# FFT and SwiGLU kernel: first-batch loads over two queues, sign and weight passes on ScalarE, and extra TensorE work between the first stages

## The chip, the cores and the metric

The kernel runs on one core of one Trainium2 chip. The metric is the device time of that core in microseconds (us). Times are medians over fast runs. Every run of a kernel was compared with runs of the kernel before on the same chip in the same rounds. Below, `before` is the kernel before the change and `after` is the changed kernel.

The first profile that I had of `before` shows TensorE at half its rate: consecutive 512-column matmuls start 443 ns apart in it.

## The reference

```python
# x: (8, 3008, 256) f32;  w_gate, w_val: (256, 1536) f32;  w_out: (1536, 256) f32
X = np.fft.fft(np.fft.fft(x, axis=1), axis=2).real.astype(np.float32)
t = X.reshape(8 * 3008, 256)
g = t @ w_gate
out = ((g / (1 + np.exp(-g))) * (t @ w_val)) @ w_out      # (24064, 256) f32
```

## The kernel before

The kernel computes the sequence transform as matmuls with cosine and sine tables (`Tab`). It multiplies the transform over the feature dimension into the gate and value weights instead of applying it to the data. So the start-up has to make two things before the main stage can begin: the first transformed tile (`Pt`, `Qt`) and the first transformed weights (`Wp`, `Wq`, `Wm`). The main stage is then one long sequence of gate, value and output matmuls.

The tables have symmetries, so rows of x are first added to and subtracted from their mirror rows. "Rising" rows are read in order and "falling" rows are their mirrors. Of the first batch, set A has 128 rows of each kind in four column groups (`XA`, rising in 0:4 and falling in 4:8). Set C has the remaining 60 in two halves of the partitions (`XC0`), plus the two single rows that are loaded by one small DMA. A permutation matmul in f32 (`place`) lines the rising rows up with the falling ones. VectorE then makes the sums and differences (`sums`), GpSimd folds A's columns (`fold_d`) and ScalarE rounds them to bf16 (`EOb`). TensorE multiplies with the tables (`half_folded` for A, `unfolded` for C).

The loads, on two queues. `nc.sync` is the engine that the profile calls SP:

```python
    nc.vector.memset(zero, 0.0)
    nc.vector.memset(sel, 0.0)
    nc.scalar.activation(halfpi, zero, AF.Silu)
    xf = XC0.rearrange("p a q d -> p (a q d)")
    nc.scalar.copy(xf, zero.to_broadcast([P, xf.shape[1]]))
    q.dma_start(out=XA3[:, 0:4, :], in_=up_block(0, 1, P))
    for a in (3, 2, 1, 0):
        q.dma_start(out=XA3[:, 4 + a, :], in_=down_set(0, a, JA, LA, NA))
    for hi, eng in ((1, nc.scalar), (0, q)):
        eng.dma_start(out=XC3[64 * hi:64 * hi + NCR, 0:2, :],
                      in_=rows_at(0, 2 * (P + 1) - 1 + 2 * hi * R, [[2 * D, NCR], [R * D, 2], [1, 2 * D]]))
        for a in range(2):
            eng.dma_start(out=XC3[64 * hi:64 * hi + NCR, 2 + a, :],
                          in_=down_set(0, 3 - 2 * hi - a, JC, LC, NC_))
    q.dma_start(out=XC0[NCR:64 + NCR + 1:64, 0:2, 1],
                in_=rows_at(0, 0, [[2 * R * D, 2], [R * D, 2], [1, D]]))
# ... then four small DMAs on SP that copy zeros within XC
```

The opening matmuls, the passes over the tables and the tables of the feature transform:

```python
    for i in range(4):
        ps = psO.tile([P, T], F32, name="o")
        for j in range(12):
            nc.tensor.matmul(ps[:, 0:P], sel, sel, start=True, stop=True)
# ...
    def weigh(lo, hi):
        vts(Tab[:, 1, 1, :, lo:hi], Tab[:, 1, 1, :, lo:hi], scalar1=wC, scalar2=None, op0=Alu.mult)

    def opposite(ch):
        vts(Tab[:, ch, :, :, NCE:NOO - 1], Tab[:, ch, :, :, GH + 1:NCE], scalar1=-1.0, scalar2=None, op0=Alu.mult)
# ...
    def d_tables():
        magnitude(rad, rrd)
        nc.scalar.activation(CD, rad, AF.Sin, scale=-scd, bias=halfpi)
        nc.scalar.activation(SDt, rrd, AF.Sin, scale=-scd, bias=zero)
        nc.scalar.activation(CD[:, :, 0:1], CD[:, :, 0:1], AF.Copy, scale=0.5)
```

Placing, sums, folds, first table matmuls and the weight products:

```python
    def place(X, put, n, pools):
        pss = []
        for a in range(n):
            pool, nm = pools[a % len(pools)]
            ps = pool.tile([P, 2, D], F32, name=nm)
            nc.tensor.matmul(ps.rearrange("p q d -> p (q d)"), put, X[:, a].rearrange("p q d -> p (q d)"),
                             start=True, stop=True)
            pss.append(ps)
        return pss

    def sums(S, k, X, pss):
        n = len(pss)
        for a in range(n):
            down = X[:, 7 - a] if n == 4 else X[:, 2 + a]
            vtt(S[:, k, a], pss[a], down[:, ::-1, :], op=(Alu.add, Alu.subtract)[k])
# ...
    def half_folded(eo, a0):
        for q in range(2):
            for a in range(a0, a0 + 2):
                dst, rhs = set_cols(acc[eo][q], Tab[:, 0, q, eo], a)
                nc.tensor.matmul(dst, EOb[:, eo, a, q, :], rhs, start=(a == 0), stop=False, skip_group_check=True)
# ...
    def fold_d(eo, a0):
        s_ = SA[:, eo, a0:a0 + 2]
        ptt(EOA[:, eo, a0:a0 + 2, :, 0:P], s_[:, :, :, P:0:-1], s_[:, :, :, P:D], op=(Alu.add, Alu.subtract)[eo])
        nc.scalar.copy(EOb[:, eo, a0:a0 + 2], EOA[:, eo, a0:a0 + 2, :, 0:P])
# ...
    def transform_w(fc, gv, k, ps):
        dst, tab = ((Wp, CD), (Wq, SDt))[k]
        src = W0[gv] if fc == 0 else Wraw[gv][:, :, (fc - 1) * T:fc * T]
        fs = slice(fc * T, (fc + 1) * T)
        for no in range(2):
            nc.tensor.matmul(ps, tab[:, no, :], src[:, no, :], start=(no == 0), stop=(no == 1))

        def copies():
            if k:
                nc.scalar.copy(dst[:, gv, fs], ps)
                if fc == 1:
                    nc.scalar.activation(Wm[:, gv, fs], ps, AF.Copy, scale=m2)
                else:
                    pts(Wm[:, gv, fs], dst[:, gv, fs], scalar1=m2, scalar2=1.0, op0=Alu.mult, op1=Alu.mult)
            else:
                nc.vector.tensor_copy(dst[:, gv, fs], ps)
        return copies
```

The order in which the start-up is written:

```python
    psA = place(XA, putA, 4, ((psG, "g"), (psV, "v")))
    sums(SA, 0, XA, psA)
    opposite(0)
    for a in (0, 2):
        fold_d(0, a)
    sums(SA, 1, XA, psA)
    start_acc(0)
    for a in (0, 2):
        half_folded(0, a)
        fold_d(1, a)
    psC = place(XC0, putC, 2, ((psO, "o"),))
    load_w(1)
    d_tables()
    weigh(0, NCE)
    opposite(1)
    sums(SC, 0, XC0, psC)
    halves(SBc, SC, 0)
    start_acc(1)
    for a in (0, 2):
        half_folded(1, a)
    hd = tp.tile([P, 2, 2, 1], F32, name="hd")
    ptt(hd, SA[:, 0, 0:2, :, 0:1], SA[:, 0, 2:4, :, 0:1], op=Alu.add)
    heads(nc.gpsimd, hd[:, 0], hd[:, 1], CEa)
    nc.gpsimd.tensor_copy(EOA[:, 0, :, :, P:P + 1], SA[:, 0, :, :, 0:1])
    heads(nc.gpsimd, SC[:, 0, 0, :, 0:1], SC[:, 0, 1, :, 0:1], CEc)
    sums(SC, 1, XC0, psC)
    halves(SBc, SC, 1)
    nc.vector.memset(SDt[:, :, 0:1], 1.0)
    load_w(2)
# ...
    def weights0(gv):
        for k in range(2):
            ps = psO.tile([P, T], F32, name="o")
            fn = transform_w(0, gv, k, ps)
            if gv and not k:
                nc.scalar.copy(Wp[:, gv, 0:T], ps)
            else:
                fn()

    unfolded(0, SBc)
    transform(0, 0, (0,), acc)
    weights0(0)
    for q in range(2):
        row0(0, q, acc[1][q])
    unfolded(1, SBc)
    transform(0, 0, (1,), acc, lambda: weights0(1))
```

## Time and profile before

| | before |
|---|---|
| time, median of fast runs | 626.35 us |
| first profile (TensorE at half rate): span | 1250.8 us |
| second profile (full rate; the same kernel, run later as a control): span | 624.9 us |
| first gate matmul of the main stage, second profile | 28.21 us |
| TensorE busy, second profile | 97% |

These lines are of the page of the first profile of `before`: its span, the busy time of each engine, and the TensorE clock that was granted in 40 equal slices of the span, in tenths.

```profile
span 1250.8 us, 12575 instructions
...
PE 1243.1 (99%) x4068; PEld 583.1 (47%) x4068; DVE 604.0 (48%) x1045; ACT 561.4 (45%) x996; POOL 454.1 (36%) x421
...
PEclk9999999999999999999999999999999998555555
```

The span is twice the timed median, and consecutive 512-column matmuls start 443 ns apart. The clock row says nines for the most part (the mean granted clock is 0.931), so it does not show this state. The prediction was made from this profile, by halving TensorE's times.

The control run of `before` gave a profile at full rate. Everything below compares it with the full-rate profile of `after`.

```profile
span 624.9 us, 12515 instructions
...
PE 606.9 (97%) x4008; PEld 394.6 (63%) x4068; DVE 570.2 (91%) x1045; ACT 524.5 (84%) x996; POOL 453.7 (73%) x421
...
PEclk8799999999999999999999999999999999999999
```

(The page counts 60 matmuls fewer than weight loads, where most other pages count the same: some matmul records are missing, here after the start-up. The page of `after` lacks 60 too.) Two slices of the start-up are not at full clock. The timeline of TensorE shows what happens there. The columns are start (us), duration (us), engine, line, operation, output and inputs, shapes and count; the bracket is the idle time just before and what ended it. This is `before`, full rate.

```profile
12.86 0.81 PE L440 MATMUL v<-Tab,EOb 128*128 128x377 bf16 x2 [2.75 <-ACT EOb L453]
...
17.44 3.75 PE L403 MATMUL o<-XC,putC 128*128 128x512 f32 x4 [1.89 <-DMA XC<-in_x_dram]
20.99 0.84 PE L440 MATMUL v<-Tab,EOb 128*128 128x377 bf16 x2
...
22.74 0.48 PE L440 MATMUL g<-Tab,EOb 128*128 128x377 bf16 x2
...
28.21 0.37 PE L871 MATMUL g<-Pt,Wp 128*128 128x480 bf16 x1
```

The placing of C (L403) waited 1.89 us for a DMA and then took 3.75 us. From 12.3 to 22.6 us TensorE ran at half rate: a pair of table matmuls takes 0.84 us there and 0.48 us afterwards.

Which DMA did C's placing wait for? This is the timeline of SP's queue (SPq: time in which SP issues DMAs) in the same profile.

```profile
6.38 0.40 SPq L245 DMA_DIRECT2D XC<-in_x_dram  x1
7.35 5.11 SPq L248 DMA_DIRECT2D XC<-in_x_dram  x2
12.51 0.59 SPq L250 DMA_DIRECT2D XC<-in_x_dram  x1
```

Why it waited for just that load can be read from the packed trace, which holds the semaphore on which each load signals its landing. In those of `before` and `after` the twelve loads of A and C use eight semaphores. The ninth to the twelfth load each use the semaphore of an earlier load again, and SP waits for that semaphore before each of them. In `before` the single rows are the twelfth load. In the new order they are the eighth, the last one that needs no such wait.

VectorE's timeline in the same profile:

```profile
12.00 0.38 DVE L340 TENSOR_SCALAR Tab<-Tab 128x752 bf16<-128x752 bf16 x1
...
14.89 1.27 DVE L337 TENSOR_SCALAR Tab<-Tab,wC 128x754 bf16<-128x754 bf16 x1
...
19.53 0.69 DVE L412 TENSOR_TENSOR SC<-o,XC 128x512 f32<-128x512 f32 x1 [2.75 <-PE o L403]
```

The sign and weight passes (L340, L337) stand between the sums (L412). Yet VectorE then stood idle for 2.75 us before C's first sum, because of the placing. In this order the passes were not what C's sums waited for.

### The profile page before, as it was taken

How to read it: one execution, taken by the hardware profiler on the slowest of the kernel's cores; microseconds unless marked ns; L12 is line 12 of the kernel's file. 1: busy time of each engine (PE TensorE's matmuls, PEld its weight loads, DVE VectorE, ACT ScalarE, POOL GpSimd, SP SyncE). 2: the span in 40 equal slices, each digit the busy share in tenths (PEclk: the TensorE clock that was granted, in tenths of full speed). 3: DMA queues.
4: the chain of work that ended last, by engine and by line, in shares of the span. 5: the costliest groups of instructions: out<-in, count | busy, mean ns of one | idle time of the engine just before them, and what ended most of it. 6: DMA issues, size and time to landing. Idle time of an engine off the chain costs nothing.

```text
span 1250.8 us, 12575 instructions
## 1 busy us (share of the span) xinstructions
PE 1243.1 (99%) x4068; PEld 583.1 (47%) x4068; DVE 604.0 (48%) x1045; ACT 561.4 (45%) x996; POOL 454.1 (36%) x421
## 2 busy tenths in 40 slices
PE   9999999999999999999999999999999999999998
PEld 4334444444444444444444444444444444545465
DVE  6543234445444554445444544545544455555552
ACT  4433223444444445444454444544445444555552
POOL 6535212343342444523434334343343221332231
PEclk9999999999999999999999999999999998555555
DMA  8312321213013002121021100103000000101011
GB/s 179 56 28 69 78 71 46 70 43 72 28 34 77 26 27 67 51 73 47 18 73 42 30 22 17 48 25 90 22 21 27 17 30 22 31 26 31 29 34 39
DMA packets 50237, 57.39 MB, mean 46 GB/s; under 512 B 7170, under 2 KB 37226, under 8 KB 50154
## 3 DMA queue, kind: packets, MB, share of 16 engines
q1 hardware_dynamic: 46701, 53.73, 16.0%
q0 software_dynamic: 3184, 2.36, 1.3%
q10 hardware_dynamic: 285, 0.49, 0.2%
q8 instruction: 32, 0.52, 0.2%
q14 instruction: 35, 0.29, 0.1%
HBM read 29.39 MB, written 24.65 MB: 43 GB/s over the span
## 4 chain that ended last, share of the span: by engine, by line
PE 99%; issue 1%; ACT 0%; POOL 0%; DVE 0%; ACTq 0%
PE o L1077 40%; PE g L871 28%; PE v L871 22%; PE o L1236 2%; PE g L1236 2%; PE o L461 1%; PE o L281 0%; PE g L549 0%; PE o L549 0%; PE v L403 0%; PE o L403 0%; PE g L403 0%; PE g L447 0%; PE v L447 0%; PE g L440 0%
## 5 line engine op out<-in xcount | busy, mean ns | idle before, releaser
L1030 POOL TENSOR_TENSOR hm<-sv 128x1024 bf16<-128x1024 f32 (+2 forms) x126 | 234.0, 1857 | 691.7 <-DVE sv L1023 293.8
L1077 PE MATMUL o<-Wo,hp 128*128 128x256 bf16 (+1 forms) x1140 | 315.9, 436 | 0.0
L1077 PE MATMUL o<-Wo,hm 128*128 128x256 bf16 (+2 forms) x1140 | 312.2, 433 | 0.7 <-ACT ev L1083 0.7
L1023 DVE SCALAR_TENSOR_TENSOR sv<-es,v 128x512 f32<-128x512 f32 (+2 forms) x252 | 170.5, 677 | 238.2 <-PE v L871 224.8
L1077 PEld LDWEIGHTS <-hp 128*128 128x128 bf16 (+1 forms) x1140 | 168.6, 148 | 186.0 <-issue 131.0
L1077 PEld LDWEIGHTS <-hm 128*128 128x128 bf16 (+2 forms) x1140 | 163.3, 144 | 196.2 <-issue 140.6
L939 ACT ACTIVATE sp<-g 128x512 f32<-128x512 f32 (+2 forms) x189 | 111.1, 588 | 214.5 <-PE g L871 213.8
L871 PE MATMUL v<-Pt,Wp 128*128 128x512 bf16 (+2 forms) x288 | 187.8, 652 | 0.0
L871 PE MATMUL g<-Pt,Wp 128*128 128x512 bf16 (+2 forms) x288 | 187.7, 652 | 0.0
L871 PE MATMUL g<-Qt,Wq 128*128 128x512 bf16 (+2 forms) x288 | 186.5, 654 | 0.0
L1009 ACT ACTIVATE sv<-g 128x512 f32<-128x512 f32 (+2 forms) x189 | 118.6, 628 | 112.7 <-PE g L871 111.9
L1033 DVE TENSOR_TENSOR hp<-sp,v 128x512 bf16<-128x512 f32 (+2 forms) x249 | 166.8, 671 | 3.0 <-ACT sp L1006 2.6
L871 PE MATMUL g<-Qt,Wm 128*128 128x512 bf16 (+2 forms) x225 | 148.2, 659 | 0.0
L964 DVE SCALAR_TENSOR_TENSOR es<-bc,w,v 128x512 f32<-128x512 bf16 (+2 forms) x126 | 92.6, 735 | 91.0 <-PE v L871 90.8
L962 ACT COPY es<-v 128x512 f32<-128x512 f32 (+2 forms) x126 | 72.7, 577 | 118.6 <-PE v L871 117.9
L871 PEld LDWEIGHTS <-Wp 128*128 128x128 bf16 x576 | 84.0, 146 | 82.8 <-issue 51.7
L871 PE MATMUL v<-Qt,Wq 128*128 128x512 bf16 (+2 forms) x162 | 106.2, 655 | 0.0
L871 PE MATMUL v<-Qt,Wm 128*128 128x512 bf16 (+2 forms) x162 | 106.2, 655 | 0.0
L871 PEld LDWEIGHTS <-Wq 128*128 128x128 bf16 x450 | 65.7, 146 | 80.5 <-issue 60.2
L1001 DVE SCALAR_TENSOR_TENSOR sg<-sg,g 128x512 f32<-128x512 f32 (+2 forms) x63 | 42.6, 676 | 105.3 <-PE g L871 105.3
L915 ACT ACTIVATE v<-bc,w 128x512 f32<-128x512 bf16 (+2 forms) x126 | 85.4, 678 | 6.3 <-DVE hp L1033 6.3
L871 PEld LDWEIGHTS <-Wm 128*128 128x128 bf16 x387 | 57.0, 147 | 58.9 <-issue 39.5
(176 smaller groups left out, 796.5 us busy)
## 6 DMA issues: line engine op xcount, KB each, us to landing
out_dram<-ev SPq DMA_DIRECT2D x96, 128.0 KB
XA<-in_x_dram SPq DMA_DIRECT2D x32, 256.0 KB
XA<-in_x_dram SPq DMA_DIRECT2D x112, 64.0 KB
XC<-in_x_dram SPq DMA_DIRECT2D x30, 120.0 KB
XC<-in_x_dram SPq DMA_DIRECT2D x105, 32.0 KB
bc<-br SPq DMA_DIRECT2D x19, 128.0 KB
St<-Fc SPq DMA_DIRECT2D x14, 128.5 KB
out_dram<-ev SPq DMA_DIRECT2D x12, 120.0 KB
```

The lines of the kernel that those rows point to most:

```text
L871: nc.tensor.matmul(ps[:, :n], Wt[:, gv, fs], src[:, :n], start=start, stop=stop, skip_group_check=True)
L915: nc.scalar.activation(T_[kv][:, :w], bc[t][:, :w], AF.Copy, scale=w0[:, 1, f:f + 1])
L939: nc.scalar.activation(T_[ksp][:, :w], T_[kg][:, :w], AF.Silu)
L962: nc.scalar.copy(T_[kes][:, :w], T_[kv][:, :w])
L964: nc.vector.scalar_tensor_tensor(T_[kes][:, :w], bc[t][:, :w], w0[:, 1, f:f + 1], T_[kv][:, :w], op0=Alu.mult, op1=Alu.add)
L1001: nc.vector.scalar_tensor_tensor(T_[kgm][:, :w], T_[keg][:, :w], 2.0, T_[kg][:, :w], op0=Alu.mult, op1=Alu.subtract)
L1009: nc.scalar.activation(sv()[:, f % 2, w - 1::-1, 1], T_[kgm if by_dve else kg][:, :w], AF.Silu)
L1023: nc.vector.scalar_tensor_tensor(sv()[:, f % 2, w - 1::-1, 0], T_[kes][:, :w], 2.0, T_[kv][:, :w], op0=Alu.mult, op1=Alu.subtract)
L1030: nc.gpsimd.tensor_tensor(hts_(t)[1][:, f - 1:f + 1, :w], sv()[:, :, :w, 1], sv()[:, :, :w, 0], op=Alu.mult)
L1033: nc.vector.tensor_tensor(hts_(t)[0][:, f, :wp], T_[ksp][:, :wp], T_[kv][:, :wp], op=Alu.mult)
L1077: nc.tensor.matmul(st["ps"][:n, j, :], hts[t][minus][:, f, c:c + n], Wo[:, f, :], start=(f == 0), stop=(f == nF - 1))
L1236: nc.tensor.matmul(st[q][:, cols], l, r_, start=(i == 0), stop=(i == len(mms) - 1), skip_group_check=True)
```

## The change

The intent was to shorten the start-up. The change has five parts.

1. **Two queues for A**: half of A's falling rows are issued by ScalarE, half by SP.
2. **C's order**: all of C's rows go through SP's queue, first the rising blocks, then the single rows, then the falling sets.
3. **ScalarE passes**: signs, weights and the magnitude of an angle move from VectorE to ScalarE. The tables of the feature transform (`d_tables`) move ahead of the first rounding copies.
4. **Warm**: 40 opening matmuls instead of 48, 20 more after the placing of A. Half of A's first table products now come after the placing of C, where all came before it.
5. **Early weights**: the first weight products come before the last table products. Their evictions come before the third weight load on GpSimd.

```diff
-    nc.scalar.activation(halfpi, zero, AF.Silu)
+    q.dma_start(out=XA3[:, 0:4, :], in_=up_block(0, 1, P))
+    for a, eng in ((3, nc.scalar), (1, nc.scalar), (2, q), (0, q)):
+        eng.dma_start(out=XA3[:, 4 + a, :], in_=down_set(0, a, JA, LA, NA))
+    nc.scalar.activation(w0[:, 0, 0:1], zero, AF.Silu)
     xf = XC0.rearrange("p a q d -> p (a q d)")
     nc.scalar.copy(xf, zero.to_broadcast([P, xf.shape[1]]))
-    q.dma_start(out=XA3[:, 0:4, :], in_=up_block(0, 1, P))
-    for a in (3, 2, 1, 0):
-        q.dma_start(out=XA3[:, 4 + a, :], in_=down_set(0, a, JA, LA, NA))
-    for hi, eng in ((1, nc.scalar), (0, q)):
-        eng.dma_start(...)                      # C: a rising block, then
-        for a in range(2):                      # two falling sets, per half
-            eng.dma_start(...)
+    for hi in range(2):
+        q.dma_start(...)                        # C: rising blocks
     q.dma_start(out=XC0[NCR:64 + NCR + 1:64, 0:2, 1], ...)   # single rows
+    for hi in range(2):
+        for a in range(2):
+            q.dma_start(...)                    # C: falling sets
@@ the opening matmuls
-        for j in range(12):
+        for j in range(10):
@@ passes (iotas, m2, sgn and wC are also made earlier: left out here)
     def opposite(ch):
-        vts(Tab[:, ch, :, :, NCE:NOO - 1], Tab[:, ch, :, :, GH + 1:NCE], scalar1=-1.0, ...)
+        nc.scalar.activation(Tab[:, ch, :, :, NCE:NOO - 1], Tab[:, ch, :, :, GH + 1:NCE], AF.Copy, scale=-1.0)
+    def weigh_ce():
+        nc.scalar.activation(Tab[:, 1, 1, :, 0:NCE], Tab[:, 1, 1, :, 0:NCE], AF.Copy, scale=wC)
     def d_tables():
-        magnitude(rad, rrd)
+        nc.scalar.activation(rad, rrd, AF.Abs)
@@ the order
     psA = place(XA, putA, 4, ((psG, "g"), (psV, "v")))
+    warm(20)
     sums(SA, 0, XA, psA)
     opposite(0)
+    d_tables()
     for a in (0, 2):
         fold_d(0, a)
     sums(SA, 1, XA, psA)
     start_acc(0)
+    half_folded(0, 0)
+    psC = place(XC0, putC, 2, ((psO, "o"),))
+    half_folded(0, 2)
+    weigh_ce()
+    opposite(1)
     for a in (0, 2):
-        half_folded(0, a)
         fold_d(1, a)
-    psC = place(XC0, putC, 2, ((psO, "o"),))
     load_w(1)
-    d_tables()
-    weigh(0, NCE)
-    opposite(1)
     sums(SC, 0, XC0, psC)
     ...
     for a in (0, 2):
         half_folded(1, a)
+    nc.vector.memset(SDt[:, :, 0:1], 1.0)
+    wts0 = [...]                                # transform_w of the first weights
     ...
     halves(SBc, SC, 1)
+    for fn in wts0:
+        fn()                                    # their evictions
     load_w(2)
@@ the first transforms
-    weights0(0)
-    transform(0, 0, (1,), acc, lambda: weights0(1))
+    transform(0, 0, (1,), acc)
```

More of the change, by code (lines that the diff above doesn't have):

```diff
@@ L237 @@
     nc.vector.memset(sel, 0.0)
-    nc.scalar.activation(halfpi, zero, AF.Silu)
+    q.dma_start(out=XA3[:, 0:4, :], in_=up_block(0, 1, P))
+    for a, eng in ((3, nc.scalar), (1, nc.scalar), (2, q), (0, q)):
+        eng.dma_start(out=XA3[:, 4 + a, :], in_=down_set(0, a, JA, LA, NA))
+    nc.scalar.activation(w0[:, 0, 0:1], zero, AF.Silu)
     xf = XC0.rearrange("p a q d -> p (a q d)")
     nc.scalar.copy(xf, zero.to_broadcast([P, xf.shape[1]]))
-    q.dma_start(out=XA3[:, 0:4, :], in_=up_block(0, 1, P))
-    for a in (3, 2, 1, 0):
-        q.dma_start(out=XA3[:, 4 + a, :], in_=down_set(0, a, JA, LA, NA))
-    for hi, eng in ((1, nc.scalar), (0, q)):
-        eng.dma_start(out=XC3[64 * hi:64 * hi + NCR, 0:2, :],
-                      in_=rows_at(0, 2 * (P + 1) - 1 + 2 * hi * R, [[2 * D, NCR], [R * D, 2], [1, 2 * D]]))
-        for a in range(2):
-            eng.dma_start(out=XC3[64 * hi:64 * hi + NCR, 2 + a, :],
-                          in_=down_set(0, 3 - 2 * hi - a, JC, LC, NC_))
+    for hi in range(2):
+        q.dma_start(out=XC3[64 * hi:64 * hi + NCR, 0:2, :],
+                    in_=rows_at(0, 2 * (P + 1) - 1 + 2 * hi * R, [[2 * D, NCR], [R * D, 2], [1, 2 * D]]))
     q.dma_start(out=XC0[NCR:64 + NCR + 1:64, 0:2, 1],
                 in_=rows_at(0, 0, [[2 * R * D, 2], [R * D, 2], [1, D]]))
+    for hi in range(2):
+        for a in range(2):
+            q.dma_start(out=XC3[64 * hi:64 * hi + NCR, 2 + a, :],
+                        in_=down_set(0, 3 - 2 * hi - a, JC, LC, NC_))
     X3c = XC.rearrange("p a q d -> p (a q d)")
@@ L266 @@
     nc.gpsimd.iota(putA, pattern=[[-LA, NA], [1, LA]], base=JA - 1, **iota)
+    nc.gpsimd.iota(df, pattern=[[-1, P]], base=P, **iota)
+    nc.gpsimd.iota(pcol2, pattern=[[0, 1]], base=P, channel_multiplier=1, allow_small_or_imprecise_dtypes=True)
     def more_iotas():
@@ L273, in more_iotas @@
             nc.gpsimd.memset(putC[:, pm:pm + 1], float(pm))
-        nc.gpsimd.iota(df, pattern=[[-1, P]], base=P, **iota)
-        nc.gpsimd.iota(pcol2, pattern=[[0, 1]], base=P, channel_multiplier=1, allow_small_or_imprecise_dtypes=True)
     for i in range(4):
         ps = psO.tile([P, T], F32, name="o")
-        for j in range(12):
+        for j in range(10):
             nc.tensor.matmul(ps[:, 0:P], sel, sel, start=True, stop=True)
@@ L313 @@
     vts(putA, putA, scalar1=pcol, scalar2=None, op0=Alu.is_equal)
+    nc.vector.memset(EOf[:, 1, :, P:P + 1], 0.0)
+    vts(m2, pcol, scalar1=0.0, scalar2=-2.0, op0=Alu.not_equal, op1=Alu.mult)
+    vts(sgn, half, scalar1=1.0 / 32, scalar2=1.0, op0=Alu.mult, op1=Alu.add)
+    vts(wC, pc, scalar1=float(LC - 1), scalar2=-0.5, op0=Alu.is_equal, op1=Alu.mult)
+    vts(wC, wC, scalar1=1.0, scalar2=None, op0=Alu.add)
     sc = 2.0 * math.pi * (1.0 - 2e-7)
@@ L339, in opposite @@
     def opposite(ch):
-        vts(Tab[:, ch, :, :, NCE:NOO - 1], Tab[:, ch, :, :, GH + 1:NCE], scalar1=-1.0, scalar2=None, op0=Alu.mult)
+        nc.scalar.activation(Tab[:, ch, :, :, NCE:NOO - 1], Tab[:, ch, :, :, GH + 1:NCE], AF.Copy, scale=-1.0)
+    def weigh_ce():
+        nc.scalar.activation(Tab[:, 1, 1, :, 0:NCE], Tab[:, 1, 1, :, 0:NCE], AF.Copy, scale=wC)
     def load_w(fc):
@@ L382 @@
     vts(putC, putC, scalar1=pcol, scalar2=None, op0=Alu.is_equal)
-    nc.vector.memset(EOf[:, 1, :, P:P + 1], 0.0)
     nc.vector.memset(sel[0:1, :], 1.0)
-    vts(m2, pcol, scalar1=0.0, scalar2=-2.0, op0=Alu.not_equal, op1=Alu.mult)
-    vts(sgn, half, scalar1=1.0 / 32, scalar2=1.0, op0=Alu.mult, op1=Alu.add)
-    vts(wC, pc, scalar1=float(LC - 1), scalar2=-0.5, op0=Alu.is_equal, op1=Alu.mult)
-    vts(wC, wC, scalar1=1.0, scalar2=None, op0=Alu.add)
     scd = 2.0 * math.pi / D * (1.0 - 2e-7)
     def d_tables():
-        magnitude(rad, rrd)
+        nc.scalar.activation(rad, rrd, AF.Abs)
         nc.scalar.activation(CD, rad, AF.Sin, scale=-scd, bias=halfpi)
@@ L424, with warm @@
     acc = [[None, None], [None, None]]
+    def warm(n):
+        ps = psO.tile([P, T], F32, name="o")
+        for i in range(n):
+            nc.tensor.matmul(ps[:, 0:P], sel, sel, start=True, stop=True)
     def start_acc(eo):
@@ L501 @@
         half_folded(1, a)
+    nc.vector.memset(SDt[:, :, 0:1], 1.0)
+    wts0 = []
+    for gv in range(2):
+        for k, (pool, nm) in enumerate((((psV, "v"), (psG, "g")), ((psO, "o"), (psO, "o")))[gv]):
+            wts0.append(transform_w(0, gv, k, pool.tile([P, T], F32, name=nm)))
     hd = tp.tile([P, 2, 2, 1], F32, name="hd")
@@ L508 @@
     halves(SBc, SC, 1)
-    nc.vector.memset(SDt[:, :, 0:1], 1.0)
+    for fn in wts0:
+        fn()
     load_w(2)
@@ L559, in products, with transform @@
         return res + [(BBc[:, q, eo, k, :], Tab[:, 1, q, (eo + k) % 2, NOO:NTAB], slice(0, G)) for k in range(2)]
-    def transform(b, part, eos, given=None, between=None):
+    def transform(b, part, eos, given=None):
         n = NCE if part == 0 else G
@@ L597, in transform @@
         for t, eo, off, s0, w, minus in sorted(todo, key=lambda v: v[0:2]):
-            if t and between:
-                between()
-                between = None
             put(eo, pq_tiles(t)[eo][:, off:off + w], s0, w, minus)
@@ L607 @@
     first_tile = {(b, part): tile_of(b * H + part * 2 * G) for b, part in jobs}
-    def weights0(gv):
-        for k in range(2):
-            ps = psO.tile([P, T], F32, name="o")
-            fn = transform_w(0, gv, k, ps)
-            if gv and not k:
-                nc.scalar.copy(Wp[:, gv, 0:T], ps)
-            else:
-                fn()
     unfolded(0, SBc)
     transform(0, 0, (0,), acc)
-    weights0(0)
     for q in range(2):
```

## The prediction

> **What bounds the kernel.** The page's header shows a span of 1250.8 us, but the timed median is 626.36 us: the profile is a half-speed picture of TensorE. In the timeline, 512-column matmuls start 443 ns apart (median), although the clock row says 9 tenths. [...] So I halve TensorE's times and keep the others. Then the busy table (DVE 604 us, ACT 561 us) says that VectorE and ScalarE are nearly as full as TensorE in a timed run. The main part, from the first gate matmul (35.1 us in the timeline), streams 1.37 million columns[...], untouched by the change. Only the start-up can change: 35 us in the profile (the chain of waits is nearly all PE), an estimated 24 to 30 us in a timed run, where other chains decide.
>
> **What the change does, with trace durations.**
> - Rows: half of A's falling rows go to ScalarE's queue, so the last lands earlier (10.55 us before, by the landings), but they share the DMA engines with the 1 MB rising block that the placing needs (landed at 6.16 us). I expect that block 0.5 to 1.5 us later, the last falling row 1 to 2 us earlier, C's last rows (16.4 us before) 2 to 4 us earlier: they no longer wait behind a semaphore in SP's queue.
> - VectorE loses 0.93 us of signs, 1.27 us of weights and 0.28 us of magnitude between the sums; ScalarE gains about 0.9 us per sign or weight pass (a 128x754 ScalarE pass took 0.91 us) and 0.4 us. C's sums start about 1.5 us sooner, but ScalarE's D tables now precede the first rounding copy of A, about 1 to 2 us late.
> - POOL: two iotas (0.37 us) move ahead of the angles; its four folds (1.1 us each) run about 0.4 us later.
> - TensorE: 48 warming matmuls become 40, 20 are added after the placing; [...] in a gap (14.2 to 16.8 in the chain of waits).
> - The first weights' products (1.89 us per four, half that warm) precede the last tables' products; their evictions leave the path between first and second transform (about 1 us of ScalarE and VectorE work).
>
> **Critical path.** I estimate that the first gate matmul starts 1 to 2 us earlier in a timed run: C's sums and the weight evictions help, the later rising block and ScalarE's longer queue take some back. Holding TensorE's clock may give 0 to 3 us more; [...] I think the clock mostly held already.
>
> **Prediction: 624.2 us, 620.5 to 627.2 in 8 of 10.** Faster by over 2%: 0.015; within 2%: 0.97; slower by over 2%: 0.015.
>
> **What would show it.** The falling rows land before 9 us, the rising block after 6.5; VectorE has no sign or weight pass between sums; ScalarE's first rounding copy follows the D tables; no weight product between the first two transforms; in the half-speed profile, start-up changes by under 2 us, since TensorE fills it.
>
> **What would make it wrong.** If TensorE was cold through the start-up of the timed runs, the added matmuls save up to 5 us. If ScalarE becomes the start-up's longest chain, or contention delays the rising block by over 2 us, the gain vanishes.

The forecast came to 624.2 us, 2.2 us below the timed 626.36 us. It rests on the estimated 1 to 2 us at the first gate matmul; the 0 to 3 us for the clock stood beside it as a possibility. Halving TensorE's times rests on the span (1250.8 us against the timed 626.36 us). "Warm" and "cold" mean full and half rate. The traces give these figures: 512-column matmuls start 443 ns apart in the first profile and 216 ns in the full-rate ones, so by an estimate from the 216 ns 1.37 million columns take 578 us; four products of the first weights take 1.89 us in the first profile and 0.86 us from start to start in the full-rate one of `before`; the 48 opening matmuls start 115 ns apart on average in the first profile, so 12 more are an estimated 1.4 us.

## More of the kernel before

The small DMA of the single rows (L250) was issued last, at 12.51 us, and landed at 17.31 us. SP was held up before it, as the chain of waits over the first 30 us shows (start, duration, what):

```profile
4.05 7.53 DMA XC<-in_x_dram
...
11.60 0.86 SPq L248
...
12.51 0.59 SPq L250
```

A rising load of C that ScalarE issued at 4.05 us, after it had filled the tile with zeros, landed at 11.58 us. Only then did SP issue its second falling load and, after it, the single rows.

## The result, and the profile after

| | before | after |
|---|---|---|
| median of fast runs | 626.35 us (625.74 to 627.19) | 623.81 us (623.35 to 623.96) |
| ratio, 95% interval | | 0.9957 (0.994 to 0.9975) |
| span of the full-rate profile | 624.9 us | 621.6 us |
| first gate matmul | 28.21 us | 23.47 us |

A ratio is the mean time of one kernel's fast runs over the mean of the other's of the same rounds, so it is not quite the ratio of the medians. The result is the same within 2%, and 0.4% faster.

This is the page of `after`, the same lines as before.

```profile
span 621.6 us, 12538 instructions
...
PE 604.1 (97%) x4020; PEld 394.0 (63%) x4080; DVE 568.3 (91%) x1042; ACT 526.8 (85%) x999; POOL 453.6 (73%) x421
...
PEclk9999999999999999999999999999999999999999
```

The busy times hardly moved. TensorE is busy 97% of both spans. The clock row is now full in the first two slices also.

TensorE's timeline of `after`:

```profile
12.67 0.49 PE L450 MATMUL v<-Tab,EOb 128*128 128x377 bf16 x2 [0.50 <-ACT EOb L463]
...
13.33 1.88 PE L408 MATMUL o<-XC,putC 128*128 128x512 f32 x4
...
19.18 0.59 PE L471 MATMUL o<-W,CD 128*128 128x512 bf16 x2 [1.00 <-DVE Wp L481]
...
23.47 0.37 PE L876 MATMUL g<-Pt,Wp 128*128 128x480 bf16 x1
24.58 0.36 PE L876 MATMUL g<-Qt,Wq 128*128 128x480 bf16 x1 [0.74 <-DVE Qt L603]
```

C's placing starts at 13.33 us, not 17.44. It waits for nothing and takes 1.88 us, not 3.75. So it ends at 15.21 us where it ended at 21.19 us.

SP's queue in `after`:

```profile
5.37 0.82 SPq L246 DMA_DIRECT2D XC<-in_x_dram  x2
6.23 0.61 SPq L248 DMA_DIRECT2D XC<-in_x_dram  x1
7.00 4.05 SPq L252 DMA_DIRECT2D XC<-in_x_dram  x4
```

The single rows (L248 here) are issued at 6.23 us instead of 12.51, and have landed by about 12.8 us instead of 17.31. The landing times of all the rows, from the transfers in the two traces:

| landed at (us) | before | after |
|---|---|---|
| A's rising block | 6.29 | 7.25 |
| A's last falling rows | 11.30 | 10.35 |
| C's two rising blocks | 11.58, 13.61 | 11.40, 12.49 |
| C's single rows | 17.31 | about 12.8 |
| C's last falling rows | 16.64 | 16.43 |

The chain of waits of `after`, over the first 30 us, now runs through C's falling rows instead of the single rows:

```profile
9.34 0.84 SPq L252
...
10.22 6.21 DMA XC<-in_x_dram
...
16.55 0.71 DVE SC L417 x2
...
22.33 13.06 DMA XA<-in_moe_w_val_dram
```

SP still waits for a semaphore: it issues a falling load of C (9.34 us) only when one of A's falling loads, issued by ScalarE, has landed (9.32 us), and the load that follows lands at 16.43 us. VectorE's timeline says the same from the other side:

```profile
13.49 0.68 DVE L417 TENSOR_TENSOR SA<-v,XA 128x512 f32<-128x512 f32 x1
...
15.69 0.69 DVE L417 TENSOR_TENSOR SC<-o,XC 128x512 f32<-128x512 f32 x1 [1.52 <-DMA XC<-in_x_dram]
```

C's first sum comes 3.84 us earlier than in `before` (15.69 against 19.53), and what it waits for is data, not the placing.

The two profiles differ by 4.74 us at the first gate matmul, but by only 3.3 us in their spans. I followed the lead of `after` through the main stage, by the starts of equally numbered instructions of one VectorE group (`hp`, one per block of work). The lead is 4.49 us from 60 to 222 us, 3.74 us at 282, 3.42 us at 364 and 3.29 us from 446 us to the end. Most of the loss is at one place, about 250 us. These lines are VectorE's and TensorE's timeline of `after` there.

```profile
251.12 0.75 DVE L969 SCALAR_TENSOR_TENSOR es<-bc,w,v 128x512 f32<-128x512 bf16 x1 [1.30 <-PE o L1082]
...
251.92 0.38 PE L876 MATMUL v<-Qt,Wq 128*128 128x512 bf16 x1 [0.62 <-DVE es L969]
```

VectorE waits for 1.30 us and TensorE then for 0.62 us. The profile puts VectorE's wait down to a matmul, but the broadcast row `bc` that the instruction reads was issued by SP at 247.72 us and landed at about 251.0 us. So I read this as a wait for that load. In `before`, VectorE waits 0.56 us for `bc` there and TensorE does not stand still. I did not test it by an experiment, and the smaller losses near 304 and 416 us stay unexplained.

### The profile page after: what moved, and what is told of

It reads as the page before. It is cut to its first block, busy times and chain, and to the rows that moved or that the text cites. A ratio compares the mean times of both kernels' runs of the same rounds, so it can differ in the third digit from the quotient of the medians.

```text
span 621.6 us, 12538 instructions
## 1 busy us (share of the span) xinstructions
PE 604.1 (97%) x4020; PEld 394.0 (63%) x4080; DVE 568.3 (91%) x1042; ACT 526.8 (85%) x999; POOL 453.6 (73%) x421
## 4 chain that ended last, share of the span: by engine, by line
PE 88%; DMA 4%; DVE 3%; ACT 2%; issue 2%; POOL 0%; ACTq 0%; SPq 0%; DVEq 0%
PE o L1082 38%; PE g L876 25%; PE v L876 20%; DMA XA<-in_moe_w_val_dram 2%; PE g L1241 2%; PE o L1241 2%; DMA XA<-in_x_dram 1%; DMA XC<-in_x_dram 1%; DVE sv L1028 1%; DVE hp L1038 1%; DVE es L969 0%; PE o L567 0%; PE g L567 0%; ACT sv L1014 0%; ACT ev L1088 0%
## 5 line engine op out<-in xcount | busy, mean ns | idle before, releaser
L1082 PE MATMUL o<-Wo,hm 128*128 128x256 bf16 (+2 forms) x1140 | 169.3, 273 | 1.4 <-ACT ev L1088 0.7
L1082 PE MATMUL o<-Wo,hp 128*128 128x256 bf16 (+1 forms) x1140 | 169.6, 273 | 0.6
L1082 PEld LDWEIGHTS <-hm 128*128 128x128 bf16 (+2 forms) x1140 | 111.6, 98 | 63.2 <-issue 2.4
L1082 PEld LDWEIGHTS <-hp 128*128 128x128 bf16 (+1 forms) x1140 | 112.0, 98 | 60.0 <-issue 0.9
L876 PE MATMUL g<-Pt,Wp 128*128 128x512 bf16 (+2 forms) x282 | 105.6, 375 | 0.2
L876 PE MATMUL v<-Pt,Wp 128*128 128x512 bf16 (+2 forms) x279 | 104.5, 375 | 0.5
L876 PE MATMUL g<-Qt,Wq 128*128 128x512 bf16 (+2 forms) x248 | 92.4, 374 | 1.3 <-DVE Qt L603 0.7
L876 PE MATMUL g<-Qt,Wm 128*128 128x512 bf16 (+2 forms) x222 | 83.1, 374 | 0.6
L1088 ACT COPY ev<-o 128x512 f32<-128x512 f32 x90 | 54.4, 605 | 10.8 <-PE o L1082 5.9
L876 PE MATMUL v<-Qt,Wm 128*128 128x512 bf16 (+2 forms) x162 | 60.7, 375 | 2.3 <-DVE hp L892 2.3
```

Of the source, the lines that this page charges most:

```text
L876: nc.tensor.matmul(ps[:, :n], Wt[:, gv, fs], src[:, :n], start=start, stop=stop, skip_group_check=True)
L1082: nc.tensor.matmul(st["ps"][:n, j, :], hts[t][minus][:, f, c:c + n], Wo[:, f, :], start=(f == 0), stop=(f == nF - 1))
L1088: nc.scalar.copy(ev[:, 0:len(pair), :], st["ps"][:, 0:len(pair), :])
```

## The experiments

Four theories were open.

- **Loads**: the gain comes from C's rows arriving earlier, and the other parts add little.
- **Clock**: the gain comes from keeping TensorE at full rate through the start-up.
- **Passes**: the gain comes from freeing VectorE.
- **Weights**: the gain comes from the early weight products, or is cut by the later third weight load.

All runs below gave correct results. They were made in three groups, each with its own 11 fast runs of `before` on the same chip (medians 626.59, 626.24 and 625.91 us). Where the first submission of a run did not reach a chip, it was submitted again with a 2 after its name; this holds for four of them.

| run | based on | ratio to before (95%) | median us | C's placing: start, duration | first gate matmul |
|---|---|---|---|---|---|
| aa_before | before, unchanged | 1.0001 (0.9987 to 1.0015) | 626.63 | 17.44, 3.75 | 28.21 |
| only_c_order | before + part 2 | 0.9959 (0.9946 to 0.9972) | 623.53 | 14.69, 1.88 | 23.74 |
| only_two_queues | before + part 1 | 0.9978 (0.996 to 0.9995) | 624.02 | 16.75, 3.51 | 27.24 |
| only_loads2 | before + parts 1, 2 | 0.9964 (0.9952 to 0.9976) | 623.89 | 14.60, 1.88 | 25.24 |
| loads_scalar | before + 1, 2, passes | 0.9945 (0.993 to 0.996) | 622.23 | 14.56, 1.88 | 23.63 |
| only_warm2 | before + warm | 1.0001 (0.9989 to 1.0013) | 626.41 | 16.89, 3.49 | 27.36 |
| undo_warm | after - warm | 0.995 (0.9936 to 0.9964) | 623.4 | 14.38, 1.88 | 24.09 |
| undo_two_queues | after - part 1 | 1.0001 (0.9979 to 1.0023) | 626.71 | 14.36, 2.90 | 25.47 |
| undo_scalar2 | after - passes | 0.9993 (0.9978 to 1.0008) | 625.99 | 16.01, 3.42 | 26.35 |
| undo_early_weights2 | after - part 5 | 0.9945 (0.9932 to 0.9959) | 623.3 | 13.78, 1.88 | 23.84 |
| w2_first | after, weight load first | 0.9956 (0.9939 to 0.9974) | 624.29 | 14.14, 1.88 | 23.79 |
| best | after, several | 0.995 (0.9932 to 0.9969) | 622.83 | 13.95, 1.88 | 24.81 |
| after | all parts | 0.9957 (0.994 to 0.9975) | 623.81 | 13.33, 1.88 | 23.47 |

Only the ratios rest on several runs. The last two columns are of one profile each, and the profiled run need not be typical: those of `after` and only_c_order are the fastest runs of their kernels, that of only_two_queues is one of its two slow ones (626.0 us, where four of six took 623.5 to 624.3).

### aa_before: the control

No edit.

> The kernel before once more, for a profile in the fast state and for the noise. All theories: ratio 1.000 within 0.2%. The start-up estimate of the prediction expects the first gate matmul between 24 and 26 us in a full-speed profile, and the granted clock whole from about 7 us on if TensorE never went cold; if TensorE was cold in the start-up, a stretch of 3 us or more with 128x377 matmuls about 0.31 us apart instead of 0.16.

The ratio was 1.0001, so a ratio such as 0.9957 lies well outside what the same kernel gives against itself. The run also gave the full-rate profile of `before` that is shown above. TensorE's clock share was 0.52 between 13 and 23 us, and the 128x377 matmuls started 0.31 us apart there (0.16 us in `after`), so the belief in the prediction that "the clock mostly held already" was wrong for this profile. The first gate matmul came at 28.21 us and not between 24 and 26 us as expected.

### only_c_order: part 2 alone

```diff
-    for hi, eng in ((1, nc.scalar), (0, q)):
-        eng.dma_start(...)              # rising block
-        for a in range(2):
-            eng.dma_start(...)          # falling sets
+    for hi in range(2):
+        q.dma_start(...)                # rising blocks
     q.dma_start(...)                    # single rows
+    for hi in range(2):
+        for a in range(2):
+            q.dma_start(...)            # falling sets
```

> The kernel before with C's rows in the new order on SP's queue alone; A's rows stay all on SP's queue. If C's order is the gain of the loads: as fast as the loads together (ratio 0.996), the placing of C starts 2 us or more sooner than 17.4 us. If the two queues are needed: within 0.7 us of before.

The ratio was 0.9959, as large a gain as that of the whole change. TensorE's timeline of this kernel:

```profile
12.98 0.49 PE L441 MATMUL v<-Tab,EOb 128*128 128x377 bf16 x2 [3.01 <-ACT EOb L454]
...
14.69 1.88 PE L404 MATMUL o<-XC,putC 128*128 128x512 f32 x4
...
23.74 0.37 PE L872 MATMUL g<-Pt,Wp 128*128 128x480 bf16 x1
```

The placing follows the table matmuls without a wait, at full rate, and the first gate matmul is within 0.3 us of that of `after`. The single rows landed at about 12.5 us, and C's falling sets between 12.8 and 15.26 us. So a change of order and queue among seven loads is sufficient for the gain. The edit also relieves ScalarE of three issues (4.05 to 6.57 us in `before`), a rival that I did not test apart. But its first rounding copy came no earlier (12.31 us against 12.18), nor did the first table matmul (12.98 against 12.86).

### only_two_queues: part 1 alone

```diff
     q.dma_start(out=XA3[:, 0:4, :], in_=up_block(0, 1, P))
-    for a in (3, 2, 1, 0):
-        q.dma_start(out=XA3[:, 4 + a, :], ...)
+    for a, eng in ((3, nc.scalar), (1, nc.scalar), (2, q), (0, q)):
+        eng.dma_start(out=XA3[:, 4 + a, :], ...)
@@ ScalarE's first Silu now follows these lines and writes w0: left out here
```

> The kernel before with A's falling rows on two queues alone; C's rows are issued as before, half of them from ScalarE behind its copy. If the two queues are the gain: ratio about 0.996. If C's order is the gain: within 0.7 us of before; and it may be slower by up to 1 us, since ScalarE now issues five loads before its tables.

The ratio was 0.9978 and the interval only just excludes 1. In the profile, C's placing still started at 16.75 us and ran at half rate. But the six runs are of two kinds, and the profile is of the slower kind: two took 626.0 and 626.4 us, as long as `before`, and four took 623.5 to 624.3 us, as short as with the C order. So the ratio of about half the gain is a mixture, and what happens in the faster runs is not shown.

### only_loads2: parts 1 and 2

The edits of the last two runs together:

```diff
+    for a, eng in ((3, nc.scalar), (1, nc.scalar), (2, q), (0, q)):
+        eng.dma_start(out=XA3[:, 4 + a, :], ...)
@@ C: the rows of both halves, all on q
+    for hi in range(2):
+        q.dma_start(...)                # rising blocks
     q.dma_start(...)                    # single rows
+    for hi in range(2):
+        for a in range(2):
+            q.dma_start(...)            # falling sets
```

> The kernel before with the loads of the change alone: A's falling rows on two queues, and C's rows in the new order on SP's queue. If the loads are the gain: C's rows no longer hold the placing of C back (it started at 17.4 us in the full-speed profile of before), C's sums start 2 to 2.6 us sooner than 19.5 us, and the run is 1.5 to 2.5 us faster than before. If the loads only help together with ScalarE's passes or the held clock: within 0.7 us of before.

The ratio was 0.9964. Beside 0.9959 for the C order alone, the two queues added nothing that these runs can see. The profile shows a cost that I had sized wrongly, and which the trace explains in part. This is VectorE's timeline:

```profile
11.71 1.72 DVE L341 TENSOR_SCALAR Tab<-Tab 128x752 bf16<-128x752 bf16 x1
13.34 0.68 DVE L413 TENSOR_TENSOR SA<-g,XA 128x512 f32<-128x512 f32 x1
```

And this is GpSimd's:

```profile
11.06 2.13 POOL L453 TENSOR_TENSOR EOA<-SA 128x512 f32<-128x512 f32 x2
```

The same sign pass took 0.38 us in `before` and 1.72 us here. Here it starts while GpSimd's two folds are running (11.06 to 13.19 us) and ends only after them. In `before` it started at 12.00 us, as the first fold was ending (12.15 us); the second began at 12.16 us and took 1.16 us instead of 1.09. In three profiles where the folds followed each other directly, the pass that started during them ended 0.16 to 0.23 us after the last one: it took 1.72 us here, 2.27 us (the same pass) in only_two_queues and 1.92 us (the magnitude) in only_c_order. Meanwhile a plain sum (0.68 us) is as long beside the folds as without them. Why the pass ends only after the folds and the sum does not, no view shows. The 0.38 us in `before` show that the pass can also slip in as one fold ends. The cost of such a pass is therefore not a fixed number that can be read from one profile. Even the weight pass of `before` (1.27 us) began during a fold and ended 0.21 us after it; in only_c_order, clear of the folds, it took 0.41 us.

### loads_scalar: parts 1 and 2, with the sign and weight passes on ScalarE

```diff
     def opposite(ch):
-        vts(Tab[...], Tab[...], scalar1=-1.0, scalar2=None, op0=Alu.mult)
+        nc.scalar.activation(Tab[...], Tab[...], AF.Copy, scale=-1.0)
+    def weigh_ce():
+        nc.scalar.activation(Tab[:, 1, 1, :, 0:NCE], ..., AF.Copy, scale=wC)
@@ the order
     start_acc(0)
+    weigh_ce()
+    opposite(1)
     for a in (0, 2):
         half_folded(0, a)
@@ after d_tables()
-    weigh(0, NCE)
-    opposite(1)
```

> The loads of the change in the kernel before, and the three sign and weight passes on ScalarE ahead of the last two folds' rounding; nothing else. With the loads alone the first sign pass of VectorE took 1.72 us between two folds of POOL (0.38 us in before) and the weights 1.26 us. If VectorE waits there for POOL: A's second sums start about 1.6 us sooner than 13.34 us, C's first sum near 16 us instead of 17.73 us, the first gate matmul 1 to 1.5 us sooner than 25.24 us. In time: 0.5 to 1 us faster than the loads alone if the lead holds; within 0.4 us of them if it is given back about 250 us in, as the kernel after gave back 0.75 of its 4.49 us there.

The ratio was 0.9945 with the lowest median of all, 622.23 us. Its interval overlaps with that of only_loads2 (0.9964), so the 0.2% between them are not established. The magnitude was left on VectorE in this kernel, and it met the folds in its turn:

```profile
13.20 0.68 DVE L416 TENSOR_TENSOR SA<-v,XA 128x512 f32<-128x512 f32 x1
13.79 1.65 DVE L329 TENSOR_SCALAR rad<-rrd 128x256 int32<-128x256 int32 x1
16.07 2.51 DVE L416 TENSOR_TENSOR SC<-o,XC 128x512 f32<-128x512 f32 x4 [0.63 <-ACT EOb L457]
```

That pass takes 0.28 us in `before` and 1.65 us here, where the four folds run from 11.06 to 15.28 us. It ended at 15.44 us, again with the folds.

### undo_scalar2: `after` with the passes back on VectorE

```diff
     def opposite(ch):
-        nc.scalar.activation(Tab[...], Tab[...], AF.Copy, scale=-1.0)
+        vts(Tab[...], Tab[...], scalar1=-1.0, scalar2=None, op0=Alu.mult)
     def weigh_ce():
-        nc.scalar.activation(..., AF.Copy, scale=wC)
+        weigh(0, NCE)
     def d_tables():
-        nc.scalar.activation(rad, rrd, AF.Abs)
+        magnitude(rad, rrd)
```

> The kernel after with signs, weights and magnitude back on VectorE. If moving them is part of the gain: C's first sum starts 0.5 to 1.5 us later than 15.7 us and the run is 0.5 to 1.5 us slower than the kernel after. If C's rows decide when the sums start: within 0.4 us of the kernel after.

The ratio was 0.9993: the whole gain is gone, although the C order is still there. VectorE's and ScalarE's timeline:

```profile
11.74 1.66 DVE L347 TENSOR_SCALAR Tab<-Tab 128x752 bf16<-128x752 bf16 x1
13.32 0.28 DVE L335 TENSOR_SCALAR rad<-rrd 128x256 int32<-128x256 int32 x1
...
13.64 0.51 ACT L398 ACTIVATE CD<-rad,halfpi 128x256 bf16<-128x256 f32 x1 [5.00 <-DVE rad L335]
...
14.54 1.12 ACT L463 CAST EOb<-EOA 128x512 bf16<-128x512 f32 x2
```

The change had moved the feature tables ahead of the first rounding copies. With the magnitude on VectorE, it waits behind a sign pass that takes 1.66 us beside the folds. ScalarE stands for 5.00 us until the magnitude is there, and the first rounding copy comes at 14.54 us instead of 12.02 us in `after`. TensorE's first table matmul comes at 15.20 us instead of 12.67 us. This profile also lost the clock from 15.68 us, and how much of the loss is due to that is not separated. So the passes on ScalarE seem to be needed by the order of this change. They are not needed for the gain: only_c_order has it with all passes on VectorE.

### only_warm2: the extra matmuls alone

```diff
-        for j in range(12):
+        for j in range(10):
@@
     psA = place(XA, putA, 4, ((psG, "g"), (psV, "v")))
+    warm(20)
```

> The kernel before with 40 opening and 20 added matmuls alone. In the full-speed profile of before TensorE ran at half rate from 12.9 to 22.6 us, after a gap of 2.8 us. If that half rate is on the path: with the added matmuls the 128x377 ones are 0.16 us apart from 12.9 us on, the placing of C (3.75 us) takes 1.9 us, and the run is 1 to 2 us faster than before. If other chains decide (loads, VectorE): within 0.5 us.

The ratio was 1.0001. TensorE's timeline:

```profile
12.87 0.49 PE L445 MATMUL v<-Tab,EOb 128*128 128x377 bf16 x2 [0.21 <-ACT EOb L458]
...
16.89 3.49 PE L403 MATMUL o<-XC,putC 128*128 128x512 f32 x4 [1.90 <-DMA XC<-in_x_dram]
```

The added matmuls did their local work: the table matmuls come after a gap of 0.21 us instead of 2.75 and run at full rate. But C's placing then waits 1.90 us for its rows as before, and runs at half rate. The extra matmuls did not fill this gap, which lies further down and is made by data.

### undo_warm: `after` without the extra matmuls

```diff
-        for j in range(10):
+        for j in range(12):
@@ 
-    warm(20)
```

> The kernel after without the 20 added matmuls, and with 48 opening ones again. If holding TensorE's clock is what the change brings: 1.5 to 3 us slower than the kernel after, and a stretch of matmuls at half rate in the start-up. The prediction's view (the clock mostly held already): within 0.5 us of the kernel after.

The ratio was 0.995, so nothing was lost. The half rate came in this profile from 7.4 to 10.8 us, while A was placed, and C's placing was at full rate.

### undo_two_queues: `after` with A's falling rows on SP alone

```diff
-    for a, eng in ((3, nc.scalar), (1, nc.scalar), (2, q), (0, q)):
-        eng.dma_start(out=XA3[:, 4 + a, :], ...)
+    for a in (3, 2, 1, 0):
+        q.dma_start(out=XA3[:, 4 + a, :], ...)
```

> The kernel after with the falling rows of A all on SP's queue again, C's rows as in the kernel after. If two queues help: 0.5 to 1.5 us slower than the kernel after. If the shared DMA engines take it back: the rising block lands about 0.8 us earlier (6.2 to 6.5 us instead of 7.25), the first placing starts as much earlier, and the time is the same within 0.5 us or better.

The ratio was 1.0001 with a spread of 623.86 to 628.53 us, the widest of all. This does not fit with only_c_order, which has A's rows on SP alone too and gains everything. TensorE's timeline shows two losses:

```profile
13.12 0.81 PE L450 MATMUL v<-Tab,EOb 128*128 128x377 bf16 x2 [2.20 <-ACT EOb L463]
...
21.18 0.59 PE L471 MATMUL o<-W,CD 128*128 128x512 bf16 x2 [1.13 <-DMA W<-in_moe_w_val_dram]
```

The table matmuls and most of C's placing are at half rate here, and the early weight products wait for a weight load, which landed at 21.05 us. The first comes from the clock, the second from the order of part 5. C's rows are not late here: the single rows landed at 12.55 us. Nor are A's: its placing started at 6.11 us, as soon as the rising block was there, and at 7.38 us in `after`. only_c_order has neither loss: its weight products come later, after the tables' products. The half rate cannot be the whole reason, since a run with the mean clock at 1.000 still took 626.27 us. That the wait for the weights makes the rest is not shown.

### undo_early_weights2: `after` with the weight products back between the transforms

```diff
-    wts0 = [...]                        # products before the last tables' products
@@ after halves(SBc, SC, 1)
-    for fn in wts0:
-        fn()
@@ the first transforms: weights0 of before
+    weights0(0)
-    transform(0, 0, (1,), acc)
+    transform(0, 0, (1,), acc, lambda: weights0(1))
```

> The kernel after with the first weights' products back between the two transforms. If taking them out of that path is a gain, as the prediction says: about 1 us slower than the kernel after. Rival: in the kernel after these products stand ahead of the last tables' products and wait for a weight load that lands at 19 to 21 us (16.3 in before), so undoing it costs nothing or is up to 1 us faster.

The ratio was 0.9945 beside 0.9957 for `after`. The early products bring no gain that can be seen. In `after`, TensorE waits 1.00 us in the middle of them for an eviction (line at 19.18 us above).

### w2_first: the third weight load before the evictions

```diff
     halves(SBc, SC, 1)
+    load_w(2)
     for fn in wts0:
         fn()
-    load_w(2)
```

> The kernel after, with the issue of the third weight quarter put ahead of the evictions of the first. Theory A: in the kernel after POOL issues that load at 21.6 and 22.3 us, behind two scalings that wait for ScalarE's evictions (2.4 us of waiting and 1.4 us of work), its last part lands at 35.4 us and TensorE stands 1.7 us for it; issued at about 18 us it lands 2 to 4 us earlier, the stand goes, and the run is 1 to 2 us faster than the kernel after (about 622). Rival: the DMA engines are full there anyway (busy in tenths 9 from 24 to 34 us), so the load lands less than 1 us earlier and the time stays within 0.5 us of the kernel after.

In `after` the value part of the third weights lands late, at 35.39 us (32.46 us in `before`), and TensorE waits for it. This line is from the same timeline of TensorE in `after`:

```profile
35.43 0.60 PE L471 MATMUL o<-XA,CD 128*128 128x512 bf16 x2 [0.32 <-DMA XA<-in_moe_w_val_dram]
```

The wait is 0.32 us, not the 1.7 us of the expectation. Nor were the DMA engines full throughout in `after`: their share was 0.31 from 27 to 28 us and 0.78 from 28 to 29 us, and 0.85 or more in the rest of 24 to 34 us. With the load moved up it landed at 31.99 us and this wait was gone, but just before it TensorE now waits 1.30 us for VectorE (0.70 us in `after`). The ratio was 0.9956, the same as that of `after`. Moving up the long transfer at the end of the chain of waits brought no gain that can be seen.

### best: the parts that the runs seemed to favour

`after` without the extra matmuls and without the early products (the last edits again), and with the first weight load behind the first fold, to free DMA time for C's rows:

```diff
-    load_w(0)
     ptt(rrd, rrd, prod, op=Alu.add)
@@ 
-    for a in (0, 2):
-        fold_d(0, a)
+    fold_d(0, 0)
+    load_w(0)
+    fold_d(0, 2)
```

> The kernel after without the early weights' products and without the added matmuls, and with the first weight load issued after POOL's first fold instead of ahead of all folds. If the weight load's bytes delay C's last falling rows (they land at 16.8 us and the second sum of C waits for them): these land 0.5 to 1.5 us sooner, the first gate matmul starts before 23.8 us, and the run is 0.3 to 1 us faster than the kernel after. Rival: the weights then land after 20 us and hold their products back; no faster than the kernel after.

The edit did what it was meant to do for the rows: C's last falling rows landed at 14.50 us instead of 16.43. But the second fold started only at 14.22 us, because GpSimd now issues the weight load ahead of it (12.53 to 14.20 us), so the second rounding copy came at 15.36 us instead of 12.98. A was also placed at half rate in this profile. The first weights came only at 19.4 and 20.9 us. The ratio was 0.995, no better than `after`, undo_warm or undo_early_weights2 within the intervals. No version tested is established as faster than `after`.

### A pattern in the clock, found afterwards

The clock can be read from the traces in steps of 0.2 us. In the eight full-rate profiles that show a stretch at half rate in the start-up, the granted clock is 0.50 in it, and its length is 3.41 us or two or three times that:

| run | half rate from, to (us) | length | TensorE busy in the 3.41 us before |
|---|---|---|---|
| aa_before | 12.33, 22.57 | 3 x 3.41 | 1.18 us |
| only_two_queues | 13.06, 19.89 | 2 x 3.41 | 1.06 us |
| only_warm2 | 16.58, 19.99 | 3.41 | 1.34 us |
| undo_scalar2 | 15.68, 19.10 | 3.41 | 0.48 us |
| undo_two_queues | 12.99, 16.40 | 3.41 | 1.34 us |
| undo_warm | 7.36, 10.77 | 3.41 | 1.31 us |
| w2_first | 7.69, 11.10 | 3.41 | 1.21 us |
| best | 7.18, 10.60 | 3.41 | 1.52 us |

What sets this length, the traces do not show. One idle gap alone does not tell whether the clock is lost: TensorE idled for 3.01 us in only_c_order without losing it, and for 2.20 us in undo_two_queues with losing it. Nor does the work in 3.41 us alone: ahead of the eight stretches it was 0.48 to 1.52 us, but in only_c_order TensorE was busy for only 0.40 us between 9.60 and 13.01 us, and the clock held. Within the longer stretches, TensorE was busy for 2.70 and 1.71 us in the first two parts of 3.41 us of aa_before and for 2.51 us in the first of only_two_queues, and another part at half rate followed. In the last or only part of each of the eight stretches it was busy for 3.10 us or more, and full rate followed. No rule for the clock is established by this.

The five runs with half rate during C's placing (the first five rows) are exactly those with ratios from 0.9978 to 1.0001. All others, the three with half rate during A's placing included, have ratios from 0.9945 to 0.9964. This is an association over 13 kernels with one profile each, and I made no run to force the half rate into one place or another.

Each run lists its mean granted clock. By an estimate from the table, 3.41 us at half rate cost 0.0027 of it (1.7 of 624 us), and the profiled runs agree: 0.991 with three times 3.41 us in aa_before, 0.994 with two in only_two_queues, 0.997 with one in only_warm2, 0.999 with none in the start-up of `after`. All 38 runs of `before` with a listed clock lie at 0.990 to 0.995, so the loss was not an accident of the one profile. But the clock alone does not set the time. In only_warm2 the run at 0.997 took 626.67 us, those at 0.991 to 0.993 took 626.22 to 626.68; and the runs of undo_two_queues have a mean clock of 0.997, as those of undo_warm have, with a mean time of 626.67 us against 623.49. So less time at half rate is not enough for the gain. What the clock adds to it is not separated.

## Why the prediction was right or wrong

**The time and the limit: right, the time partly by luck (see the first gate matmul below).** I predicted 624.2 us and measured 623.81. The first profile was rightly read as a half-rate picture, and halving TensorE's times gave the right view (443 ns between 512-column matmuls there, 216 ns in both full-rate profiles). With TensorE at full rate, VectorE is busy 91% of the span and ScalarE 84%. The main stage did not change in kind, and only the start-up moved. Its estimated end at 24 to 30 us in a timed run holds the 28.21 us of `before`.

**"C's last rows ... 2 to 4 us earlier: they no longer wait behind a semaphore in SP's queue": the right wait, but the wrong rows.** The reordered loads are the part that carries the gain; the C order alone gives 0.9959. (With other parts in the way it can be lost again, as in undo_two_queues and undo_scalar2.) But C's last falling rows landed at 16.43 us instead of 16.64, since SP waits again in the new order. What came earlier was the small load of the single rows, by about 4.5 us: it was the last of twelve, behind the waits for semaphores, and is now the eighth. That load and the rising blocks are inputs of the placing, on which everything of C depends. The prediction never named this load. I did not move it alone, so how much of the gain it has by itself is open.

**"Half of A's falling rows ... I expect that block 0.5 to 1.5 us later, the last falling row 1 to 2 us earlier": nearly right.** The rising block came 0.96 us later, the last falling rows 0.95 us earlier. The check "before 9 us" failed: 10.35 us. That the DMA engines are shared agrees with the profile of `after`: over the first 14 us the packets of SP's queue took 63.7% of the 16 engines' time, those of ScalarE's queue 14.0% and GpSimd's 14.4%. How the engines divide their time among the queues is not shown. Alone, this part gave 0.9978, a mixture of fast and slow runs.

**"C's sums start about 1.5 us sooner" from freeing VectorE: wrong reason.** They started 3.84 us sooner, but in `before` VectorE was idle for 2.75 us ahead of them. The passes were not on the path. On ScalarE they took 0.82 to 0.92 us each, and the magnitude 0.42 us, in `after`. And their cost on VectorE, which I took as 0.93, 1.27 and 0.28 us, is not fixed: beside GpSimd's folds the sign pass took up to 2.27 us and the magnitude 1.92 us, and the weights, at 1.27 us, had ended 0.21 us after a fold already. Where other parts of the change pull an order tighter, the move to ScalarE seems to be needed (undo_scalar2: 0.9993).

**"ScalarE's D tables now precede the first rounding copy of A, about 1 to 2 us late": wrong.** The first rounding copy came at 12.02 us in `after` and 12.18 us in `before`. ScalarE was idle for 2.19 us ahead of it in `before`, and the tables fit into that time.

**"I think the clock mostly held already": wrong.** In the full-rate profile of `before` the clock was halved for 10.2 us, three times 3.41 us. TensorE stood idle for 2.75 us before its first matmul in that stretch. The listed clocks show a loss in all 38 runs of `before`. My own condition for failure, that TensorE was cold through the start-up, was met for that stretch. But what I attached to it, that "the added matmuls save up to 5 us", did not happen: alone they gave 1.0001, and without them the change gave 0.995. That early rows brought the clock of C's placing back is not shown: early rows and a full-rate placing went together in eight profiles, but in undo_two_queues and undo_scalar2 the rows were early and the placing was at half rate.

**"The evictions leave the path between first and second transform (about 1 us)": not shown.** Without this part the ratio was 0.9945 against 0.9957, with overlapping intervals.

**"The first gate matmul starts 1 to 2 us earlier": too small.** It was 4.74 us earlier in the two profiles, of which 3.29 us remained at the end and 2.54 us appear in the medians. The 0 to 3 us that I allowed for the clock would cover it, but I did not count on them. So two errors cancelled: I had sized the start-up's gain too low, and had not expected that over 1 us of it is lost again later, 0.75 us of it at the place that I read as a wait for a load.

**Start-up "changes by under 2 us" at half rate: not tested.** The profile of `after` fell at full rate.

## What to carry to other kernels

When one engine's queue issues several loads, the last small one can hold the whole start-up. In `before` SP issued it at 12.51 us, after the load ahead of it had waited for a landing at 11.58 us; the loads from the ninth on reused the semaphores of earlier ones. Look up when each load of a stage was issued, on what it waited and which instruction needs it before you look at engine work. Matmuls that were added to hold TensorE's clock did not help here (1.0001 alone), where the 1.90 us gap that followed was made by a late load: remove that wait first. And take the cost of a VectorE pass from the place where it will stand, since passes that took 0.28 and 0.38 us in `before` took up to 1.92 us (only_c_order) and 2.27 us (only_two_queues) beside GpSimd's folds.
